# A dilated and sliding attention with a squared-ReLU FFN on one core: another order of the first loads, of the first batch's preparation and of the second layer's first groups

## Chip, core and metric

The kernel runs on 1 core of a Trainium2 chip. The metric is the device time of one execution in microseconds (us). Before the change the median of 5 runs is 316.51 us (316.03 to 317.87).

## What is computed

Two stages follow each other. First attention over 8 batches, 8 heads, 576 positions of 64 elements. Heads 0 to 3 see a plain causal window of 32 positions; heads 4 to 7 see 32 positions at a distance of 4 ("dilated"). Then the 4608 x 512 result goes through an FFN with 2048 hidden units.

```python
rel = pos[:, None] - pos[None, :]
mask_plain = (rel >= 0) & (rel < 32)
mask_dil = (rel >= 0) & (rel < 128) & (rel % 4 == 0)
attn = softmax(where(mask, q @ k.T / 8, -1e9))       # heads 0-3 plain, 4-7 dilated
x = (attn @ v) as 4608 tokens x 512
out = (relu(x @ w_in) ** 2) @ w_out                  # w_in 512 x 2048, w_out 2048 x 512
```

## The kernel before

**Units of work.** A head pair is called `e` (0 and 1 plain, 2 and 3 dilated). Batches 0 and 1 are cut in two parts (part 0: positions 0 to 255, part 1: the rest). Attention writes x transposed into the ring `xT`, where the FFN reads it. The FFN runs in tiles of 256 tokens (the first four) and then 512. `ffn_groups` (line 645) makes the groups of a tile: first-layer groups (`mm1`, line 656, matmuls on line 667, ReLU on ScalarE on line 678, square on VectorE on line 679), and second-layer groups (`g2`, line 691, matmuls on line 699). A second-layer group is named by an output row block `m` of 128 tokens and a `part` 0 to 3; part c multiplies four blocks of the hidden units by chunk c of `w_out_sb`, so the group waits for that chunk's load. When part 3 of an m is done, ScalarE copies the sum out of PSUM (line 705) and SyncE issues the store (line 641).

**Who sets the order.** Everything is ordered by hand, and each engine runs its instructions in that order. The text `PROGRAM` (line 21) is cut at each "|"; the piece before the first bar runs ahead of all groups, and each later piece runs behind one group of the list `groups` (line 802). The codes:

- `L0:q…`, `L0:v…`, `L0:i0` to `i3`, `L0:o0` to `o3`: loads, all issued by GpSimd (POOL) into one queue. `L0:q001` is q and k of batch 0, part 0, pairs 0 and 1; `i` is a quarter of w_in (line 753), `o` a chunk of w_out (line 758). `L0:v1d`, `L0:v1p`, `L0:v1r` are the values of part 1: `d` the dilated pairs (line 184), `p` the plain pairs (line 178), and `r` the last 64 positions of the dilated pairs, block 8 (two small loads on line 197).
- `w22`, `W14`: so many matmuls on a zeroed tile (`idle`, line 465) of 256 and 128 columns. Nothing reads their results.
- `T C B S E P D L X M` with e and part: batch 0's attention (`first_step`, line 469): transposes of q and k on TensorE (T, line 495), copies out of PSUM (C), masks added by a matmul (B, line 536), scores (S, line 555), exponential on ScalarE (E, line 560), product with the values (P, line 586), sums for the denominator (D, line 602), logarithm and its exponential on ScalarE (L and X, lines 609 and 612), the product into `xT` on VectorE (M, line 619).
- `1q2`, `2v2` and the like: a step of a later batch (`step`, line 434). q and k are transposes into the PSUM pool `ps_a` of two buffers (line 235) with copies into `qT` or `kbd` (lines 248 to 265; q of a plain pair is copied by ScalarE, the others by VectorE); v copies dilated values from the staging tile to `vbd` on VectorE (line 207); a and b are scores, o and p the product with the values, whose result VectorE scales into `xT` on line 428.

**Around the change.** In the first piece P of the dilated pairs (part 0) stands ahead of the transposes of their part 1. `groups` is reordered for the first two tiles: first-layer groups of both in turns, and from group 16 on the second layer of tile 0 (m 0 parts 0 to 3, then m 1 parts 0 to 3), then of tile 1. Behind group 1 stand `P21 P31`, which need the block-8 values.

Of the kernel before, what the change touches and what calls it, by code (L numbers as in the profile page):

```python
# [18 lines left out]


PROGRAM = (
    "L0:q001 L0:q023 L0:q101 L0:q123 L0:v0d L0:v0p L0:i0 L0:v1d L0:i1 L0:v1p L0:v1r L0:i2 L0:i3 L0:o0 "
    "L1:q00123 L0:o1 L0:o2 L0:o3 w22 T00 C00a T10 C10a B00 B10 W2 S00 E00 W3 S10 E10 W14 T20q W9 T20k C20v T30 "
    "C30v B20 B30 W3 S20 E20 W3 S30 E30 T01 C01v T11 C11v B01 B11 W2 S01 E01 P20 P30 D20 D30 T21 C21v S11 L20 "
    "X20 E11 T31 C31v M20 B21 B31 P00 P10 D00 D10 L00 X00 M00 S21 E21 S31 E31 W8 | | P21 P31 D21 D31 L21 X21 "
    "M21 L31 X31 M31 | | P01 P11 D01 D11 L01 X01 M01 L11 X11 M11 | | | | | | | | | | | | z | | y L1:v0dp "
    "L1:q10123 L1:v1dpr | | | | L2:q00123 L2:q10123 1q1 1q3 | 1q2 | 1k2 | 1k1 1v3 | 1a2 | 1v2 1k0 1q0 | 1o2 | "
    "1a0 1a1 | 1k3 1o0 1o1 | 1a3 1Q0 | 1K0 1o3 | 1Q1 1K1 | 1Q2 | 1b0 | | 1Q3 1K2 L2:vwpdr L3:q00123 L3:q10123 "
    "| L2:x | | 2q0 | | 2k0 1V2 | 1b2 1p0 | 1b1 1V3 1K3 | | 1p2 1p1 | 2a0 1b3 | 2k1 2o0 2b0 1p3 | 2q1 2k2 L3:x "
    "| | 2q2 2p0 L3:vwpdr 2a1 | | | 2b1 | 2v2 2o1 2q3 2a2 | | 2p1 | 2k3 | 2b2 2o2 | 2v3 | 2a3 2p2 L4:q10123 | "  # L30
    "2b3 | 3k1 2o3 3q1 | | 3a1 L4:q00123 2p3 | 3k0 3k2 | | 3o1 | | | 3q0 3v2 | | | | 3a0 | 3b1 3k3 | | | 3p1 "
    "L4:x 3q2 L4:vwpdr | | 3b0 | 3a2 3q3 3o0 4k0 | | | 3o2 3b2 | | 3p0 3v3 | 4q1 3a3 | 3p2 4q2 4q0 | L5:q10123 "
    "3b3 | 3o3 | 4k1 | | L5:q00123 3p3 4k2 4k3 4a0 L5:vwpdr | | | 4b0 | | 4q3 | | 4o0 | | | 4a2 4v2 | 4b2 | "
    "4a3 L5:x 4a1 | 4o2 | | | 4p2 L6:q00123 4v3 | | 4b1 | | 4p0 | | 4p1 | 5q0 5k0 | 4b3 | | | | 4o1 | | 5k2 "
    "L6:q10123 4o3 | 5q2 5k1 | | 4p3 | 5q1 |"
)


# [25 lines left out]
def kernel(  # L64
# [36 lines left out]
    NF = DFF // P  # L101
# [690 lines left out]
    G = 2 * NF  # L792
# [5 lines left out]
    groups, steps = [], []  # L798
# [2 lines left out]

    head = groups[:G]
    groups[:NF] = [head[y] for y in (0, 1, 2, 3, 16, 17, 18, 19, 4, 5, 20, 21, 6, 7, 22, 23)]
    groups[NF:G] = head[8:16] + head[24:32]
    for b in range(5, B):
        at = {"a": (-2, 8), "b": (0, 8), "o": (3, 8), "p": (6, 8), "v": (-4, 8)}
        at = {**({"k": (-9, 4), "q": (-9, 4)} if b > 5 else {}), **at}
# [50 lines left out]
```

## Time and profile before

| | |
|---|---|
| median of 5 runs | 316.51 us |
| the profiled execution's own time | 316.51 us |
| its span in the profile | 314.7 us |
| outside the span | 1.8 us |
| TensorE busy | 301.4 us, 96% of the span |
| VectorE, ScalarE, GpSimd busy | 201.1, 194.1, 87.3 us |
| granted TensorE clock | 1.00 in every slice |

Times in the profile count from the start of the span. PE is TensorE, DVE VectorE, ACT ScalarE, POOL GpSimd, SP SyncE. In the timeline a line gives the start, the duration, engine, source line and operation, and in brackets how long the engine had been idle and what ended that. In the chain of waits a line gives what the end was waiting on at that time.

When the loads of the queue were issued and when they landed, by the trace's answers for each issue (us):

| load | issued | landed |
|---|---|---|
| last of q and k of batch 0 | 5.68 | 12.4 |
| dilated values, part 0 | 6.31, 6.92 | 12.6, 13.5 |
| plain values, part 0 | 7.55 to 10.93 | 13.6 to 14.2 |
| w_in 1st quarter | 11.78 | 17.2 |
| dilated values, part 1 | 12.70, 13.3 | 17.5, 18.0 |
| w_in 2nd quarter | 13.88 | 21.3 |
| plain values, part 1 | 14.63 to 16.7 | 21.5 to 22.4 |
| block-8 values (`v1r`) | 17.46, 18.1 | 22.5, 22.6 |
| w_in 3rd quarter | 18.65 | 26.3 |
| w_in 4th quarter | 21.59 | 28.9 |
| w_out chunk 0 | 22.33 | 31.3 |
| q and k of batch 1, part 0 | 22.86, 23.56 | 33.3, 34.7 |
| w_out chunks 1, 2, 3 | 24.2, 24.8, 25.3 | 36.4, 38.9, 41.4 |

### The profile page before, as it was taken

To read this page: it belongs to the slowest core of one execution; us is meant where nothing else is said; L and a number is where in the kernel's file an instruction comes from. 1 tells how busy PE (TensorE), PEld (TensorE's weight loads), DVE (VectorE), ACT (ScalarE), POOL (GpSimd) and SP (SyncE) were. 2 spreads that over 40 slices of the span, in tenths; PEclk is the share of its full clock that TensorE was granted. 3 is DMA by queue.
4 is the path that set the end of the run, shared out by engine and by line. 5 is a ranking of instruction groups with operands and counts; after the bars stand their busy time and mean duration, and the time that the engine had idled before them with its cause. 6 is when DMAs were issued, how large, how long until landed. Compare 5 with 4: busy or idle time off the path is not lost.

```text
span 314.7 us, 6843 instructions
## 1 busy us (share of the span) xinstructions
PE 301.4 (96%) x2582; PEld 190.2 (60%) x2614; DVE 201.1 (64%) x641; ACT 194.1 (62%) x416; POOL 87.3 (28%) x136
## 2 busy tenths in 40 slices
PE   8969989999999999999999999999999999999995
PEld 5769835867855555555589655555555555445443
DVE  6335588898987987994799469956895334104400
ACT  6348526877968965686468646864686456217511
POOL 8774378455183036501361041000000000000000
PEclk9999999999999999999999999999999999999999
DMA  8999999999989999994599985602200210121022
GB/s 106 149 184 200 213 166 144 212 147 202 165 107 206 147 133 149 146 209 44 88 146 126 129 145 109 117 3 67 69 0 2 68 68 2 32 68 35 0 67 67
DMA packets 79808, 34.91 MB, mean 111 GB/s; under 512 B 49824, under 2 KB 74784, under 8 KB 79776
## 3 DMA queue, kind: packets, MB, share of 16 engines
q0 software_dynamic: 47680, 18.36, 52.8%
q1 hardware_dynamic: 31952, 15.93, 25.0%
q8 instruction: 20, 0.33, 0.5%
q10 hardware_dynamic: 144, 0.20, 0.2%
q14 instruction: 12, 0.10, 0.1%
HBM read 36.90 MB, written 9.44 MB: 147 GB/s over the span
## 4 chain that ended last, share of the span: by engine, by line
PE 78%; DMA 9%; ACT 4%; POOL 3%; issue 2%; DVE 1%; ACTq 0%; POOLq 0%
PE pf L699 36%; PE pf L667 32%; DMA w_out_sb<-in_moe_w_out_dram 5%; PE po L413 3%; DMA w_in<-in_moe_w_in_dram 2%; PE pd L415 2%; DMA qb<-in_q_dram 2%; PE pa L304 2%; PE pa L310 1%; ACT h2T L678 1%; ACT qT L248 1%; PE pa L235 1%; POOL qb L161 1%; POOL kb L161 1%; ACT rec L417 1%
## 5 line engine op out<-in xcount | busy, mean ns | idle before, releaser
L667 PE MATMUL pf<-xT,w_in 128*128 128x256 bf16 (+1 forms) x758 | 132.7, 325 | 2.0 <-DVE xT L619 0.9
L699 PE MATMUL pf<-w_out_sb,h2T 128*128 128x512 bf16 (+1 forms) x570 | 131.2, 373 | 3.0 <-DMA w_out_sb<-in_moe_w_out_dram 1.4
L667 PEld LDWEIGHTS <-w_in 128*128 128x128 bf16 x768 | 82.3, 113 | 37.0 <-issue 2.4
L678 ACT ACTIVATE h2T<-pf 128x512 bf16<-128x512 f32 x144 | 83.8, 598 | 24.6 <-PE pf L667 23.8
L699 PEld LDWEIGHTS <-h2T 128*128 128x128 bf16 x592 | 54.2, 98 | 55.2 <-issue 2.3
L679 DVE TENSOR_TENSOR h2T<-h2T 128x512 bf16<-128x512 bf16 x144 | 58.0, 423 | 40.3 <-ACT h2T L678 38.7
L705 ACT COPY osb<-pf 128x512 f32<-128x512 f32 (+1 forms) x37 | 21.2, 573 | 46.0 <-PE pf L699 45.9
L178 POOL DMA_DIRECT2D vbd<-in_v_dram x40 | 28.2, 721 | 58.5 <-PE pd L415 49.4
L428 DVE TENSOR_TENSOR xT<-po,rec 128x288 bf16<-128x288 f32 (+2 forms) x52 | 23.7, 457 | 31.3 <-ACT rec L418 30.8
L417 ACT ACTIVATE rec<-pd 128x288 f32<-128x288 f32 (+2 forms) x52 | 21.5, 414 | 23.9 <-PE pd L415 23.1
L314 ACT ACTIVATE pt<-pa 128x352 bf16<-128x352 f32 (+6 forms) x56 | 27.6, 499 | 7.9 <-PE pa L310 4.1
L418 ACT ACTIVATE rec<-rec 128x288 f32<-128x288 f32 (+2 forms) x56 | 24.9, 445 | 1.8
L413 PEld LDWEIGHTS <-vbd 128*128 128x128 bf16 x286 | 17.0, 97 | 9.9 <-issue 0.9
L248 DVE COPY qT<-xx 64x288 bf16<-64x288 bf16 x80 | 19.8, 247 | 1.1
L252 DVE COPY kbd<-xx 64x288 bf16<-64x288 bf16 x40 | 18.8, 470 | 0.6
L161 POOL DMA_DIRECT2D qb<-in_q_dram x18 | 13.0, 723 | 20.2 <-DMA xx<-qb 17.2
L413 PE MATMUL po<-pt,vbd 128*128 128x96 bf16 (+3 forms) x263 | 18.0, 198 | 0.4 <-DVE xT L428 0.3
L191 POOL DMA_DIRECT2D vd<-in_v_dram x24 | 14.6, 629 | 8.1 <-DMA kb<-in_k_dram 4.8
L415 PE MATMUL pd<-pt,mk 128*128 128x96 bf16 (+5 forms) x158 | 16.3, 203 | 0.0
L161 POOL DMA_DIRECT2D kb<-in_k_dram x18 | 12.8, 711 | 2.7 <-DMA w_out_sb<-in_moe_w_out_dram 1.8
L304 PE MATMUL pa<-qT,kbd 128*128 128x96 bf16 (+2 forms) x146 | 12.2, 201 | 0.5 <-ACT qT L248 0.5
L197 POOL DMA_DIRECT2D vbd<-in_v_dram x16 | 9.7, 609 | 10.3 <-PE pd L415 7.4
(81 smaller groups left out, 232.2 us busy)
## 6 DMA issues: line engine op xcount, KB each, us to landing
out_dram<-osb SPq DMA_DIRECT2D x18, 128.0 KB, 3.4
qb<-in_q_dram POOLq DMA_DIRECT2D x7, 320.0 KB, 8.1
kb<-in_k_dram POOLq DMA_DIRECT2D x7, 320.0 KB, 9.2
vd<-in_v_dram POOLq DMA_DIRECT2D x32, 64.0 KB, 4.8
w_in<-in_moe_w_in_dram POOLq DMA_DIRECT2D x4, 512.0 KB, 7.3
w_out_sb<-in_moe_w_out_dram POOLq DMA_DIRECT2D x4, 512.0 KB, 13.2
qb<-in_q_dram POOLq DMA_DIRECT2D x7, 256.0 KB, 7.1
kb<-in_k_dram POOLq DMA_DIRECT2D x7, 256.0 KB, 8.8
```

The costliest lines, as they stand in the source:

```text
L161: nc.gpsimd.dma_start(t[0:n, part, hs, :], src[b, hs, t0 : t0 + RES * n, :].rearrange("h (p r) d -> p h (r d)", r=RES))
L178: nc.gpsimd.dma_start(dst[rows, e, i0:i1, rows], v[b, 2 * e + hl, 64 * i0 : 64 * i1, :].rearrange("(i p) d -> p i d", p=64),)
L248: copy(qT[rows, e, :, m0 : m0 + n].rearrange("p (c j) m -> p j c m", j=2)[:, jj, :, :], src)
L314: nc.scalar.activation(pt[:, off : off + n], ps[:, 0:n], ACT.Exp, scale=SCALE)
L413: nc.tensor.matmul(oo, vb[:, e, i, :], rh, start=(x == 0), stop=(x == len(mms) - 1), skip_group_check=True)
L417: nc.scalar.activation(rec[:, 0:n], d[:, 0:n], ACT.Ln)
L418: nc.scalar.activation(rec[:, 0:n], rec[:, 0:n], ACT.Exp, scale=-1.0)
L428: nc.vector.tensor_tensor(out=tok, in0=o if o is o3 else o[:, 0:n], in1=rec if o is o3 else rec[:, 0:n], op=ALU.mult)
L667: nc.tensor.matmul(acc[u][:, nt * x + y0 : nt * x + y1], w_in_sb[piece][:, kt, c0 : c0 + 509 : 4], xT[:, kt, t0 : t0 + y1 - y0], start=(kt ...
L678: nc.scalar.activation(hv, acc[u][:, :].rearrange("p (x n) -> p x n", x=per), ACT.Relu)
L679: nc.vector.tensor_tensor(out=hv, in0=hv, in1=hv, op=ALU.mult)
L699: nc.tensor.matmul(cur[m][:, c0:c1], h2[:, f, P * m : P * m + P], w_out_sb[:, f, c0:c1], start=(f == 0), stop=(f == NF - 1),)
```

## The change

Seven edits, all of order or of number:

1. `L0:v1r` is issued with `L0:v1d`, ahead of the second quarter of w_in, and no longer behind the plain values of part 1.
2. `L1:q00123` (q and k of batch 1, part 0) is issued behind w_out's chunks 1 and 2, ahead of chunk 3.
3. `w22` becomes `w21`, `W14` becomes `W5`, `W9` becomes `W10`.
4. `T21 C21v S11 E11 T31 C31v B21 B31` come ahead of `P20 P30 D20 D30 L20 X20 M20`.
5. The second layer of tile 0 runs m 0 parts 0 and 1, m 1 parts 0 and 1, m 0 parts 2 and 3, m 1 parts 2 and 3.
6. `2v2` moves from behind group 54 to behind group 56. On VectorE its two copies then stand behind the next product on line 428 instead of ahead of the one before it.
7. `3k1` moves from behind group 62 to behind group 61; no engine's order of instructions is altered by it.

```diff
-    "L0:q001 L0:q023 L0:q101 L0:q123 L0:v0d L0:v0p L0:i0 L0:v1d L0:i1 L0:v1p L0:v1r L0:i2 L0:i3 L0:o0 "
-    "L1:q00123 L0:o1 L0:o2 L0:o3 w22 T00 C00a T10 C10a B00 B10 W2 S00 E00 W3 S10 E10 W14 T20q W9 T20k C20v T30 "
-    "C30v B20 B30 W3 S20 E20 W3 S30 E30 T01 C01v T11 C11v B01 B11 W2 S01 E01 P20 P30 D20 D30 T21 C21v S11 L20 "
-    "X20 E11 T31 C31v M20 B21 B31 P00 P10 D00 D10 L00 X00 M00 S21 E21 S31 E31 W8 | | P21 P31 D21 D31 L21 X21 "
...
-    "| | 2q2 2p0 L3:vwpdr 2a1 | | | 2b1 | 2v2 2o1 2q3 2a2 | | 2p1 | 2k3 | 2b2 2o2 | 2v3 | 2a3 2p2 L4:q10123 | "
-    "2b3 | 3k1 2o3 3q1 | | 3a1 L4:q00123 2p3 | 3k0 3k2 | | 3o1 | | | 3q0 3v2 | | | | 3a0 | 3b1 3k3 | | | 3p1 "
...
+    "L0:q001 L0:q023 L0:q101 L0:q123 L0:v0d L0:v0p L0:i0 L0:v1dr L0:i1 L0:v1p L0:i2 L0:i3 L0:o0 L0:o1 L0:o2 "
+    "L1:q00123 L0:o3 w21 T00 C00a T10 C10a B00 B10 W2 S00 E00 W3 S10 E10 W5 T20q W10 T20k C20v T30 C30v B20 "
+    "B30 W3 S20 E20 W3 S30 E30 T01 C01v T11 C11v B01 B11 W2 S01 E01 T21 C21v S11 E11 T31 C31v B21 B31 P20 P30 "
+    "D20 D30 L20 X20 M20 P00 P10 D00 D10 L00 X00 M00 S21 E21 S31 E31 W8 | | P21 P31 D21 D31 L21 X21 M21 L31 "
...
+    "2p0 L3:vwpdr 2a1 | | | 2b1 | 2o1 2q3 2a2 | | 2p1 2v2 | 2k3 | 2b2 2o2 | 2v3 | 2a3 2p2 L4:q10123 | 2b3 3k1 "
+    "| 2o3 3q1 | | 3a1 L4:q00123 2p3 | 3k0 3k2 | | 3o1 | | | 3q0 3v2 | | | | 3a0 | 3b1 3k3 | | | 3p1 L4:x 3q2 "
...
-    groups[NF:G] = head[8:16] + head[24:32]
+    groups[NF:G] = [head[y] for y in (8, 9, 12, 13, 10, 11, 14, 15)] + head[24:32]
```

## Prediction

> **What bounds the kernel now.** I read the page's busy times first. TensorE does something in 96% of the span, so only its gaps and what it has to wait for can move the end:
>
> ```profile
> PE 301.4 (96%) x2582; PEld 190.2 (60%) x2614; DVE 201.1 (64%) x641; ACT 194.1 (62%) x416; POOL 87.3 (28%) x136
> ```
>
> Then the list of what TensorE waited for in the first 60 us, and the chain of waits there:
>
> ```profile
> PE po L586 <- DMA vbd<-in_v_dram: 1.8, 1, 1.8
> PE pf L699 <- DMA w_out_sb<-in_moe_w_out_dram: 1.4, 1, 1.4
> ```
>
> ```profile
> 25.32 16.09 DMA w_out_sb<-in_moe_w_out_dram
> 41.41 0.04 issue
> 41.45 2.75 PE pf L699 x12
> ```
>
> The two largest waits are P21 for the block-8 values (20.9 to 22.7 us) and m 0 part 3 of tile 0 for w_out's chunk 3 (to 41.45 us). The chain says that only the second one sets the end: it goes from 41.41 us back along the load queue and never through the first. What happened on TensorE before 41 us matters only by what was left to do at 41.4 us. Now the timeline behind that moment:
>
> ```profile
> 41.45 2.75 PE L699 MATMUL pf<-w_out_sb,h2T 128*128 128x512 bf16 x12 [1.37 <-DMA w_out_sb<-in_moe_w_out_dram]
> ...
> 42.51 0.59 ACT L705 COPY osb<-pf 128x512 f32<-128x512 f32 x1 [4.39 <-PE pf L699]
> ...
> 44.04 0.45 PE L235 MATMUL pa<-mk,qb 80*128 80x80 bf16 x8
> ...
> 44.32 1.03 PE L699 MATMUL pf<-w_out_sb,h2T 128*128 128x512 bf16 x4
> 44.38 1.08 ACT L248 COPY qT<-pa 64x128 bf16<-64x128 bf16 x4 [1.28 <-PE pa L235]
> ...
> 45.51 0.30 PE L235 MATMUL pa<-mk,qb 80*128 80x80 bf16 x4 [0.16 <-ACT qT L248]
> ```
>
> Twelve matmuls are three groups (m 0 part 3, m 1 parts 0 and 1; 0.86 us each in the chain). Then come 1q1 and 1q3, one more group, and 1q2, which needs a `ps_a` buffer back and so waits for ScalarE's four copies of 1q1.
>
> **Part by part.**
>
> *Loads (edits 1 and 2).* The landings in the table come one behind the other from 17 us to 41 us, and the GB/s of the slices stay between 150 and 240 there: the queue is limited by what it moves. The bytes ahead of chunk 3 are the same after the change, so I take its landing at 41.4 us again. From 8.68 us on each POOL issue follows the landing of the load eight places before it (w_in's fourth quarter 21.59 after the second's 21.3; the first values of batch 1 26.56 after 26.3). With the new order the second quarter is issued at about 15.1 instead of 13.88 us, still 3 us before the loads ahead of it have landed (18.0), so no hole opens; POOL's later issues stay as far ahead of the queue as now. The block-8 values land at some 18.0 + 0.25 us (their two landings, 22.35 to 22.6) = 18.3 instead of 22.6 us, the second quarter at 21.6 instead of 21.3. Chunks 1 and 2 come 2.0 + 1.4 us earlier, near 33 and 35.5 us; q and k of batch 1 land near 38 and 39.4 us, before 1q1 wants them (42.3, below).
>
> *Fewer idle matmuls and the order of batch 0 (edits 3 and 4).* 14 idle matmuls took 0.78 us, 0.056 each. One less at the start gains nothing: the first transposes began at 5.32, and their k landed at 5.2. 9 less and 1 more are 8 x 0.056 = 0.45 us for all that follows (their q landed at 7.3, their k at 8.4 us, in time). T21, S11, T31 and B21 then run where TensorE waited 0.5 us for the values of part 0 (landed 13.5). ScalarE and VectorE set the rest, L20 to M00: D30 ends at about 14.55, then L20, X20, L00, X00 at some 0.62 us each and M00 0.69, so M00 ends near 17.85 instead of 18.79. First-layer work starts 0.9 us earlier. P21 starts at 19.5 and finds its values (18.3): the 1.8 us wait goes. Late next is w_in's second quarter: D31 ends at 20.9, u2 starts at 21.6 instead of 23.7. All that follows moves up by 2.1 us, and group 16 starts at 35.2 instead of 37.3 us.
>
> *Second layer (edit 5).* Before chunk 3 lands TensorE can now do five groups instead of three: 35.2 + 5 x 0.86 = 39.5 us. Then it waits 1.9 us for 41.4, longer than now. So all that edits 1, 3 and 4 gain is given back here; they serve only so that group 16 starts before 41.4 - 4.3 = 37.1 us, which today's 37.3 nearly does. After chunk 3 there are 2 groups fewer: 2 x 0.86 = 1.73 us by TensorE alone. But 1q1 now comes straight behind m 0 part 3, and its copies queue on ScalarE behind that block's copy-out. The copy-out starts at 42.51 as now; ScalarE's next start is 0.48 later (another copy-out at 51.11, its successor at 51.59); from there to 1q2 it is 45.51 - 44.38 = 1.13 us. So 1q2 starts at 42.51 + 0.48 + 1.13 = 44.12 instead of 45.51: **1.39 us** gained, and TensorE waits some 0.5 us in front of 1q2. Below VectorE runs almost without a pause from 1q2's copies on (45.85 to 51.8), so the shift is handed on as it is. Bounds: 1.73 if ScalarE does not hold it, 1.1 if the copy-out ends fully before the next starts (0.59) and chunk 3 comes 0.2 later.
>
> *2v2 and 3k1 (edits 6 and 7).* 3k1 alters no engine's order: nothing. For 2v2 the rows are:
>
> ```profile
> 85.13 0.60 DVE L207 COPY vbd<-vd 64x512 bf16<-64x512 bf16 x2
> ...
> 85.76 0.42 DVE L428 TENSOR_TENSOR xT<-po,rec 128x256 bf16<-128x256 f32 x1
> ...
> 86.24 0.38 PE L413 MATMUL po<-pt,vbd 128*128 128x32 bf16 x6 [0.35 <-DVE xT L428]
> ...
> 87.86 0.49 DVE L428 TENSOR_TENSOR xT<-po,rec 128x320 bf16<-128x320 f32 x1
> ...
> 88.57 0.34 PE L413 MATMUL po<-pt,vbd 128*128 128x96 bf16 x5
> ...
> 90.51 0.45 DVE L428 TENSOR_TENSOR xT<-po,rec 128x288 bf16<-128x288 f32 x1
> ...
> 91.01 0.33 PE L413 MATMUL po<-pt,vbd 128*128 128x96 bf16 x5
> ```
>
> The copies (0.63 us with their gaps) hold up the product at 85.76, whose denominators were ready at 85.48; without them TensorE's wait at 86.24 shrinks by 0.26. But the copies then run behind the product of 87.86 (87.6 after the shift), to 88.6, and 2o2 at 88.57 reads what they write: it waits about 0.35. The eight copies of 2k3 and the product of 90.51 move back by 0.35, and the matmuls of 91.01 need that product's buffer. Net +0.3 us. Bounds: -0.26 (if nothing behind is late) and +0.63 (all of it on the path). I take **+0.3**, by the chain just followed.
>
> *Sum.* 316.51 (this execution's own time, equal to the median) - 1.39 + 0.3 = **315.4 us**, 0.35% less.
>
> *The clock.* The granted clock is 1.00 in all slices, across the present gaps of 1.8 and 1.4 us. I count no loss for a 1.9 us gap. The Trainium skill, "TensorE: Matmul & The Clock Gate", section "HAM oscillation — how this bites in real kernels", speaks against longer gaps: it lets TensorE fall to half its clock when it is idle for more than about 3.4 us. By that rule the estimated 1.9 us is safe; if the gap grew past it, the next window would run at half speed, and the estimate from that page is a loss of 1.7 us, for 317.1.
>
> **The rivals.**
>
> *More comes through (314.5).* ScalarE's copies don't hold 1q2, and 2v2 gains its 0.26: 316.51 - 1.73 - 0.26 = 314.5. For it: the wait for ScalarE is only 0.16 us now. Against: the copy-out stood 1.9 us ahead of those copies and is now right in front of them.
>
> *Swallowed later (316.3).* VectorE is busy 16.6 of 18.8 us from 56 to 75 us and 21.2 of 25 from 75 to 100. If the 2v2 move costs its full 0.63, and VectorE loses as much again before the long tiles start at 94 us, 1.39 - 1.26 leaves 0.2: 316.3. Against: the chain from 45 to 75 us is mostly TensorE's own matmuls, and the loads there have slack (q of batch 2 landed at 54.8 and 58.9, used at 64.7).
>
> *Slower: chunk 3 lands late (317.4).* Place: the load queue. w_in's second and third quarters took 3.3 and 3.65 us between landings, the fourth 2.65: a weight load next to small value blocks or to q and k can cost 0.65 to 1.0 us more. If the new neighbours make two such (block 8 ahead of the second quarter, q and k ahead of chunk 3), chunk 3 lands 2.0 us later, and each us of that is a us of the end: 316.51 - 1.1 + 2.0 = 317.4. From a delay of 1.1 us on the kernel is slower than before. Against: the same loads in another order have the same neighbours in sum.
>
> **How the numbers follow.** Forecast (314.9 to 315.9): 0.50. More: 0.20. Swallowed: 0.22. Slower: 0.08. About 0.3%, 0.95 us, can be told from no change: faster means below 315.56. Of the forecast's 0.50 some 0.35 lies below that; with 0.20 and a little of the third case this is 0.57. Same: 0.15 + 0.20 = 0.36. Slower over 0.3%: 0.07, nearly all from the last rival. The range goes from the second case to the third with a margin of 0.3 for chunk 3's landing: 314.3 to 316.5.
>
> **What would show it.** After: TensorE's largest wait is in front of m 0 part 3, about 1.9 us, ending at 41.4; none at P21, a short one for w_in's second quarter near 21; the copy-out at 42.5 again; 1q2 at 44.1 behind a wait for ScalarE of about 0.5; a wait for line 207 near 87 us. The prediction is wrong if chunk 3 lands more than 0.5 us away from 41.4, if the distance from 1q2 to the span's end changes by more than 0.6 us, or if the granted clock falls anywhere.

## The result and the profile after

The changed kernel has a median of 315.95 us (46 executions, 314.09 to 319.48), the kernel before, on the same chips, 317.15 us (88 executions, 314.92 to 319.71). The ratio is 0.9963, 95% interval [0.995, 0.9975]: 0.37% or 1.2 us faster. Predicted were 315.4 us, 1.1 us less than the 316.51 us that the prediction started from; over 88 executions the kernel before has 317.15 us, so the measured 315.95 us lies above the predicted time although the difference agrees. The profiled execution of the changed kernel took 315.1 us with a span of 313.3 us, 1.4 us below that of before, with a mean granted clock of 0.999 (before 1.000).

The busy times hardly differ, so the gain must lie in gaps:

```profile
PE 301.8 (96%) x2573; PEld 190.1 (61%) x2605; DVE 200.6 (64%) x641; ACT 194.3 (62%) x416; POOL 87.3 (28%) x136
```

What TensorE waited for in the first 60 us of the changed kernel (us in total, times, longest):

```profile
PE pf L667 <- DVE xT L619: 1.3, 3, 0.8
...
PE pf L699 <- DMA w_out_sb<-in_moe_w_out_dram: 0.7, 1, 0.7
PE pf L555 <- issue: 0.6, 1, 0.6
PE pa L235 <- ACT qT L248: 0.5, 1, 0.5
...
PE pf L667 <- DMA w_in<-in_moe_w_in_dram: 0.3, 1, 0.3
```

P21's wait of 1.8 us for the block-8 values is gone, and that for chunk 3 is 0.7 instead of 1.4 us, not 1.9 as predicted. The chain of waits of the changed kernel still comes from chunk 3, and behind it from ScalarE:

```profile
25.24 16.04 DMA w_out_sb<-in_moe_w_out_dram
41.32 1.04 PE pf L699 x4
42.38 0.59 ACT osb L705
...
43.99 0.30 PE pa L235 x4
```

The timeline of the changed kernel there (one group of the second layer is four matmuls; a few records are missing from the traces, so x19 stands for the 20 of five groups):

```profile
36.19 4.48 PE L699 MATMUL pf<-w_out_sb,h2T 128*128 128x512 bf16 x19
...
41.32 1.02 PE L699 MATMUL pf<-w_out_sb,h2T 128*128 128x512 bf16 x4 [0.65 <-DMA w_out_sb<-in_moe_w_out_dram]
...
42.18 0.45 PE L235 MATMUL pa<-mk,qb 80*128 80x80 bf16 x8
42.38 0.59 ACT L705 COPY osb<-pf 128x512 f32<-128x512 f32 x1 [5.39 <-PE pf L699]
...
42.86 1.08 ACT L248 COPY qT<-pa 64x128 bf16<-64x128 bf16 x4
...
43.99 0.30 PE L235 MATMUL pa<-mk,qb 80*128 80x80 bf16 x4 [0.49 <-ACT qT L248]
```

Chunk 3 landed at 41.28 us (before 41.41). Behind it come four matmuls instead of twelve, 1q1 and 1q3, the copy-out and ScalarE's four copies, and 1q2 starts at 43.99 instead of 45.51: 1.52 us earlier. That shift is handed on: 1.51 us at group 56, 1.57 us at 2p2 (91.01 before, 89.44 after), 1.4 us at the end. From 1q2 to the end of the span it is 269.2 us before and 269.3 after.

### The profile page after: what moved, and what is told of

Read it like the earlier page. It is cut to its first block, busy times and chain, and to the rows that moved or that the text cites. A ratio compares the mean times of both kernels' runs of the same rounds, so it can differ in the third digit from the quotient of the medians.

```text
span 313.3 us, 6824 instructions
## 1 busy us (share of the span) xinstructions
PE 301.8 (96%) x2573; PEld 190.1 (61%) x2605; DVE 200.6 (64%) x641; ACT 194.3 (62%) x416; POOL 87.3 (28%) x136
## 4 chain that ended last, share of the span: by engine, by line
PE 77%; DMA 10%; ACT 5%; POOL 3%; issue 2%; DVE 2%; ACTq 0%; POOLq 0%
PE pf L699 36%; PE pf L667 32%; DMA w_out_sb<-in_moe_w_out_dram 5%; PE po L413 3%; DMA w_in<-in_moe_w_in_dram 2%; PE pd L415 2%; DMA vd<-in_v_dram 2%; PE pa L304 2%; PE pa L310 1%; ACT h2T L678 1%; ACT qT L248 1%; POOL qb L161 1%; POOL kb L161 1%; PE pa L235 1%; ACT rec L417 1%
## 5 line engine op out<-in xcount | busy, mean ns | idle before, releaser
L705 ACT COPY osb<-pf 128x512 f32<-128x512 f32 (+1 forms) x37 | 21.2, 574 | 47.0 <-PE pf L699 46.9
L252 DVE COPY kbd<-xx 64x288 bf16<-64x288 bf16 x40 | 18.8, 471 | 0.6
```

## The experiments

The theory is the prediction's: chunk 3's landing is a fixed point, work ahead of it counts only if it keeps TensorE from arriving late, and edit 5 gains by leaving less behind it. Each expectation states its rivals. Ratios are to the kernel before, run on the same chip beside it, with 95% intervals. The diffs of `PROGRAM` show only the codes around a difference, without the line breaks of the text; "..." stands for codes that are the same. In the expectations e2 is the kernel of "all but edit 5".

**Edit 5 alone** (before with the new second-layer order):

```diff
-    groups[NF:G] = head[8:16] + head[24:32]
+    groups[NF:G] = [head[y] for y in (8, 9, 12, 13, 10, 11, 14, 15)] + head[24:32]
```

> The kernel before with edit 5 alone (second layer of tile 0 in the new order). Theory A (the landing of w_out's chunk 3 at 41.3 to 41.4 us is fixed, and only what is left to do behind it moves the end): group 16 starts at 37.3 us as before, five groups end at 41.6, chunk 3 is no longer waited for or by less than 0.2 us, 1q2 starts at 44.2 instead of 45.51, and the time is 1.0 to 1.4 us (0.3 to 0.45%) below the kernel before, nearly all of the change. Theory B (the earlier preparation of batch 0 and the earlier block-8 values carry the gain): less than 0.3 us below the kernel before.

Measured: 0.9972 [0.995, 0.9993], 316.39 us against 317.36. So edit 5 brings a gain by itself. But 5 of 12 executions had a mean granted clock below 0.9975, and these had a median of 317.35 us, the others 315.86. The profiled one is of the first kind. Its windows from P21's wait on (length, then busy time and count of PE, PEld, DVE, ACT and POOL, then the granted clock, DMA share and GB/s):

```profile
20.90:22.70 1.80, 0.04 (x3) 0.05 (x1) 0.42 (x1) 0.27 (x1) 1.16 (x2) 1.00 1.35 191
22.70:24.00 1.30, 1.30 (x23) 0.94 (x24) 0.00 (x0) 0.06 (x1) 1.30 (x3) 0.63 1.09 144
24.00:25.00 1.00, 1.00 (x8) 0.76 (x7) 0.08 (x1) 0.97 (x3) 1.00 (x3) 0.50 1.15 179
25.00:26.00 1.00, 1.00 (x6) 0.74 (x5) 0.66 (x2) 0.68 (x2) 1.00 (x3) 0.50 1.22 197
26.00:27.00 1.00, 1.00 (x9) 0.83 (x7) 0.53 (x2) 0.60 (x1) 0.45 (x1) 0.77 1.31 238
```

Behind a pause of 1.8 us TensorE ran at half clock for some 3.5 us (a "dip" below). The sum had no term for that. One such stretch takes about 0.0055 off the mean clock of a span of 316 us (half of 3.5 in 316), so by this estimate a mean of 0.995 is one dip and 0.989 two.

**All but edit 5** (the changed kernel with the old line):

```diff
-    groups[NF:G] = [head[y] for y in (8, 9, 12, 13, 10, 11, 14, 15)] + head[24:32]
+    groups[NF:G] = head[8:16] + head[24:32]
```

> The changed kernel with the second layer of tile 0 in the old order. Theory A: group 16 starts at 36.2 us as after the change, three groups can be done ahead of chunk 3, the wait for chunk 3 is 41.3 - 36.2 - 2.6 = 2.5 us, 1q2 is at 45.4, and the time equals the kernel before within 0.2 us. Theory B: 1.0 us or more below the kernel before.

Measured: 1.0062 [1.0037, 1.0087], 319.56 us: slower than before, which neither theory had foreseen. 11 of 12 executions had a mean clock below 0.9975, four of them 0.989 or less. TensorE arrives early, waits long for chunk 3, and the twelve matmuls behind it are slow. Timeline, then windows, of this kernel:

```profile
41.83 4.18 PE L699 MATMUL pf<-w_out_sb,h2T 128*128 128x512 bf16 x12 [3.50 <-DMA w_out_sb<-in_moe_w_out_dram]
```

```profile
38.30:41.80 3.50, 0.03 (x1) 0.00 (x0) 3.12 (x4) 0.00 (x0) 1.35 (x2) 1.00 1.40 186
41.80:43.00 1.20, 1.17 (x6) 0.57 (x6) 0.61 (x2) 0.11 (x1) 0.92 (x2) 0.99 1.08 108
43.00:44.00 1.00, 1.00 (x4) 0.30 (x3) 0.00 (x0) 0.48 (x1) 1.00 (x3) 0.50 1.46 193
44.00:45.00 1.00, 1.00 (x4) 0.33 (x3) 0.00 (x0) 0.00 (x0) 1.00 (x2) 0.50 0.90 89
45.00:46.00 1.00, 1.00 (x6) 0.44 (x5) 0.00 (x0) 0.00 (x0) 1.00 (x3) 0.50 1.12 130
46.00:47.00 1.00, 1.00 (x12) 0.67 (x10) 0.41 (x2) 0.66 (x3) 1.00 (x3) 0.80 1.15 132
```

The same twelve took 2.75 us in the profile of before and 4.18 here.

**The clock as the cause**: the same kernel with 50 idle matmuls in that wait, which keep TensorE from pausing.

```diff
-    L1:q10123 L1:v1dpr | | | | L2:q00123
+    L1:q10123 L1:v1dpr | W50 | | | L2:q00123
```

> e2 (all edits but the new second-layer order) with 50 idle matmuls of 128 columns ahead of the group that waits for chunk 3. They write a PSUM tile that nobody reads. Clock theory (the pause of 3.5 us in front of chunk 3 let the granted clock fall to 0.50 for 3.5 us behind it, and that is why e2 took longer than the kernel before): the pause shrinks to under 1 us, the twelve matmuls behind chunk 3 take 2.75 us and not 4.18, the clock stays at 1.00, and the time falls by 1.5 to 3 us to the kernel before, 316.5 to 317.4. Rival (e2 is slow for another reason, a later landing of chunk 3 through the changed loads): the time stays within 0.5 us of e2.

Measured: 1.0013 [0.9985, 1.004], 318.04 us, 1 of 12 executions at the lower clock. That is 1.5 us less than without the idle matmuls, but above the 316.5 to 317.4 us expected. Timeline of the stretch:

```profile
41.05 2.95 PE L465 MATMUL pf<-idle 128*128 128x128 bf16 x50
43.84 2.75 PE L699 MATMUL pf<-w_out_sb,h2T 128*128 128x512 bf16 x11
```

The matmuls behind the filler are back at 2.75 us, against 4.18 without it: 1.43 us, which is nearly all of the 1.5. The rival, a late chunk 3, is out: the time fell, although in the profiled execution chunk 3 landed at 42.2 us, later than the 41.8 without the filler. The 1.0013 does not say that the other edits come to nothing, for 11 of the 19 executions of the kernel before beside it had a dip themselves. The executions without one have medians of 317.99 us with the filler and 316.85 before. Why these 1.1 us remain is not shown; the filler can cost time itself, as in the profiled execution, where it ended 1.6 us after the landing. That execution is also the one with a dip, in another place:

```profile
23.30 3.48 PE L667 MATMUL pf<-xT,w_in 128*128 128x256 bf16 x16 [1.62 <-DMA w_in<-in_moe_w_in_dram]
```

With the block-8 values ahead of it w_in's second quarter landed at 23.25 us here (21.3 in before). TensorE waited for it instead of for the block-8 values, and from 24 to 26 us the clock was 0.50.

**Edit 1 alone** (before, `L0:v1dr` ahead of the second quarter):

```diff
-    L0:v1d L0:i1 L0:v1p L0:v1r
+    L0:v1dr L0:i1 L0:v1p
```

> The kernel before with edit 1 alone (block-8 values ahead of w_in's second quarter). The prediction's chain of waits: TensorE gains 1.8 us at P21 and gives it back in front of chunk 3, time equal to the kernel before within 0.2 us. Clock theory (a pause of 1.8 us or more lets the granted clock fall to 0.50 in part of the executions, and the longer the pause the more often): the pause at P21 goes, but the one in front of chunk 3 grows from 1.4 us to 2.5 to 3.5 us, as in e2; the clock falls behind chunk 3 in most executions, with nothing left to hide it, and the time is 1 to 2 us above the kernel before.

Measured: 1.0009 [0.998, 1.0038], 318.09 us as the median of all twelve executions, of which 8 had the lower clock. The ratio leaves out the two longest (320.17 and 319.82 us, mean clock 0.989). With them the median is 0.9 us above that of before (317.16), so the expected loss of 1 to 2 us is neither shown nor excluded. In the profiled execution the dip cost little, and its timeline shows why:

```profile
39.52 1.86 PE L699 MATMUL pf<-w_out_sb,h2T 128*128 128x512 bf16 x4 [1.83 <-DMA w_out_sb<-in_moe_w_out_dram]
41.57 3.39 PE L699 MATMUL pf<-w_out_sb,h2T 128*128 128x512 bf16 x12 [0.19 <-DMA w_out_sb<-in_moe_w_out_dram]
```

Here chunks 1 and 2 come behind q and k, as in before, and TensorE pauses 1.83 us for chunk 2. Half the slow stretch (1.86 us for four matmuls, 1.02 at full clock) lies in time that would have been spent waiting for chunk 3; only 0.64 us of it (3.39 instead of 2.75 us) stands behind the landing.

**Edits 1 and 5** (before with both diffs above):

> The kernel before with edits 1 and 5 alone. Both theories: these two are the change; the time equals the changed kernel within 0.3 us (ratio to the kernel before 0.995 to 0.998). Clock theory besides: the share of executions with a granted clock under 0.997 is no larger than in the changed kernel (11 of 46) and smaller than with edit 5 alone (5 of 12, by the pause at P21). If edits 2, 3, 4, 6 carry a part, it is 0.5 us or more above the changed kernel.

Measured: 0.9953 [0.9929, 0.9977], 315.58 us, 0 of 12 executions at the lower clock. These two edits give what the whole change gives, as far as the intervals tell. Edit 5 alone (0.9972) can't be told from them by its time either; what edit 1 adds shows in the dips, 0 of 12 executions against 5 of 12. Timeline:

```profile
41.39 1.02 PE L699 MATMUL pf<-w_out_sb,h2T 128*128 128x512 bf16 x4 [0.96 <-DMA w_out_sb<-in_moe_w_out_dram]
...
44.06 0.30 PE L235 MATMUL pa<-mk,qb 80*128 80x80 bf16 x4 [0.49 <-ACT qT L248]
```

**Without edit 2** (the changed kernel, q and k of batch 1 between `L0:o0` and `L0:o1` again):

```diff
-    L0:o0 L0:o1 L0:o2 L1:q00123 L0:o3
+    L0:o0 L1:q00123 L0:o1 L0:o2 L0:o3
```

> The changed kernel with edit 2 undone (q and k of batch 1 ahead of w_out's chunks 1 and 2). Prediction: nothing, equal to the changed kernel within 0.2 us: chunks 1 and 2 land near 36.4 and 38.9 us and are wanted near 37.1 and 39.6, chunk 3 lands when it did. If chunk 2 becomes the late load, TensorE waits once more, in front of m 0 part 2, and the time is 0.3 to 0.8 us above the changed kernel.

Measured: 0.9958 [0.9933, 0.9983], 316.01 us, 0 of 12 executions at the lower clock. The wait is only split: 1.39 us in front of the first group that needs chunk 1 and 1.25 us in front of chunk 3's. Edit 2 is worth nothing that can be measured.

**Without edits 3 and 4** (the changed kernel with the old first piece):

```diff
-    w21 ... W5 T20q W10 ... E01 T21 C21v S11 E11 T31 C31v B21 B31 P20 P30 D20 D30 L20 X20 M20 P00
+    w22 ... W14 T20q W9 ... E01 P20 P30 D20 D30 T21 C21v S11 L20 X20 E11 T31 C31v M20 B21 B31 P00
```

> The changed kernel with the idle matmuls and the order of batch 0 as before (edits 3 and 4 undone). Theory A: P21 still finds its values, so group 16 starts by 36.5 us, five groups end ahead of chunk 3, and the time equals the changed kernel within 0.2 us. Theory B: it gives back 0.5 us or more. What this tells besides: the prediction had M00 0.9 us earlier by edits 3 and 4, and the trace after the change has it 0.2 us later; if those edits are worth nothing on their own, group 16 starts here at 36.0 to 36.2, no later than with them.

Measured: 0.9956 [0.9933, 0.998], 315.88 us, 2 of 12 at the lower clock. As good as the change. Group 16 even starts earlier (35.39 us, 36.19 in the changed kernel), but that follows w_in's second quarter, which landed at 21.7 us here and at 22.5 there:

```profile
35.39 4.48 PE L699 MATMUL pf<-w_out_sb,h2T 128*128 128x512 bf16 x19
42.88 1.02 PE L699 MATMUL pf<-w_out_sb,h2T 128*128 128x512 bf16 x4 [3.00 <-DMA w_out_sb<-in_moe_w_out_dram]
```

Chunk 3 landed late in this execution (42.8 us), and the pause of 3.00 us had no slow clock behind it: four matmuls in 1.02 us. With 316.77 us this execution is 0.9 us above the kernel's median: a late chunk 3 costs time by itself.

**Without edit 6** (the changed kernel, `2v2` back behind group 54):

```diff
-    | 2o1 2q3 2a2 | | 2p1 2v2 |
+    | 2v2 2o1 2q3 2a2 | | 2p1 |
```

> The changed kernel with 2v2 behind group 54 again. By the prediction it gains 0.3 us on the changed kernel. By the trace after the change (shift of 1.51 us at group 56, 1.56 behind 2p2) it loses 0.05 us, which can't be told from nothing: the wait of 0.35 us for line 428 in front of 2p1 is back, and the one of 0.19 for line 207 in front of 2o2 is gone. Also to be read: the eight copies of 2k3 on VectorE took 1.95 us before the change and 1.4 after; if it is GpSimd's issuing of loads next to them that makes them slow (it lay beside all eight before, beside six after), they take more than 1.6 us where it lies beside all of them again.

Measured: 0.994 [0.9915, 0.9964], 315.81 us, 3 of 12 at the lower clock. The interval overlaps that of the change: the move of `2v2` can't be told from nothing. The eight copies of 2k3 lay beside GpSimd's issues throughout and took 1.50 us (89.56 to 91.06), not more than 1.6: that GpSimd's issuing alone makes them slow is not borne out. The profiled execution is one with a dip. Chunk 3 landed at 43.0 us, and four matmuls behind it took 1.62 instead of 1.02 us:

```profile
43.04 1.62 PE L699 MATMUL pf<-w_out_sb,h2T 128*128 128x512 bf16 x4 [2.31 <-DMA w_out_sb<-in_moe_w_out_dram]
```

**Beyond the change.** Three kernels try what the theory suggests: bring the fixed point forward, or put work into the wait. The first loads chunk 3 ahead of q and k:

```diff
-    L0:o2 L1:q00123 L0:o3
+    L0:o2 L0:o3 L1:q00123
```

> The changed kernel with w_out's chunk 3 loaded ahead of q and k of batch 1. Theory A (TensorE waits for chunk 3 and for nothing else there): chunk 3 lands by 38 to 39.5 us, the wait in front of m 0 part 3 (0.65 us in the profiled execution, 2 to 3 us where chunk 3 landed near 43) goes, 1q1 finds q and k (landed near 41) and 1q2 comes 0.6 to 0.8 us earlier than after the change, at 43.3; no pause of TensorE over 1 us is left there, so the granted clock stays at 1.00. Time 0.6 to 1.5 us below the changed kernel. Rival C (q and k become the late load in its place): 1q1 waits for them until 41.5 or later, and the time equals the changed kernel within 0.3 us.

Measured: 0.989 [0.9844, 0.9936], 313.75 us, 0 of 6 at the lower clock. Timeline:

```profile
35.43 5.34 PE L699 MATMUL pf<-w_out_sb,h2T 128*128 128x512 bf16 x23
40.61 0.45 PE L235 MATMUL pa<-mk,qb 80*128 80x80 bf16 x8
...
42.42 0.30 PE L235 MATMUL pa<-mk,qb 80*128 80x80 bf16 x4 [0.49 <-ACT qT L248]
```

Chunk 3 landed at 38.3 us and q and k by 40.8. Six groups run through with no wait at all, and 1q2 is 1.6 us earlier than in the changed kernel. This version beats both kernels.

The second leaves the loads and moves 1q1, 1q3 and 1q2 two groups forward, ahead of chunk 3's group. `y` and `z`, zeroing on VectorE (`y` that of rows which the transposes read), move forward too:

```diff
-    | | | | | | | | | | | | z | | y L1:v0dp L1:q10123 L1:v1dpr | | | | L2:q00123 L2:q10123 1q1 1q3 | 1q2 | 1k2
+    | | | | | | | y | | | | z | | | L1:v0dp L1:q10123 L1:v1dpr | | 1q1 1q3 | 1q2 | L2:q00123 L2:q10123 | | 1k2
```

> The changed kernel with the first transposes of batch 1 moved into the wait for chunk 3 (1q1 and 1q3 behind group 19, 1q2 behind group 20), and VectorE's zeroing for batch 1 moved ahead (y behind group 9, z behind 13). Theory A: behind chunk 3's landing (41.3) only three groups are left without any wait between them; ScalarE's copies of 1q1 run ahead of the first copy-out, the wait of 0.49 us in front of 1q2 goes, and what was at 44.12 comes at 43.1: 1.0 us below the changed kernel. Rival (ScalarE's and VectorE's copies are the longer chain): 1q2 still comes late and holds chunk 3's group back; nothing gained.

Measured: 0.9907 [0.9875, 0.994], 315.01 us, 0 of 9 at the lower clock. The profiled execution, with a span of 311.2 us, was the fastest of the nine, and chunk 3 landed early in it (40.4 us), so its timeline shows the best case:

```profile
38.85 0.45 PE L235 MATMUL pa<-mk,qb 80*128 80x80 bf16 x8
...
40.33 0.30 PE L235 MATMUL pa<-mk,qb 80*128 80x80 bf16 x4 [0.16 <-ACT qT L248]
40.49 2.75 PE L699 MATMUL pf<-w_out_sb,h2T 128*128 128x512 bf16 x12
```

ScalarE's copies now lie beside groups that don't need chunk 3. The third does both, with 1q1, 1q3 and 1q2 one group forward instead of two:

```diff
-    L0:o2 L1:q00123 L0:o3
+    L0:o2 L0:o3 L1:q00123
...
-    | | | | | | | | | | | | z | | y L1:v0dp L1:q10123 L1:v1dpr | | | | L2:q00123 L2:q10123 1q1 1q3 | 1q2 | 1k2
+    | | | | | | | y | | | | z | | | L1:v0dp L1:q10123 L1:v1dpr | | | 1q1 1q3 | L2:q00123 L2:q10123 1q2 | | 1k2
```

> The two before in one: chunk 3 ahead of q and k, 1q1 and 1q3 behind group 20, 1q2 behind group 21, the zeroing ahead. Theory A: no wait over 0.3 us on TensorE from 36.2 to 44 us, state of 44.12 reached at 42.9: 1.2 us below the changed kernel where chunk 3 lands at 41.3 there, more where it lands later. Rival C: q and k land late (41.5 to 43) and 1q1 waits for them; less than 0.5 us.

Measured: 0.9896 [0.9855, 0.9937], 314.26 us, 0 of 6 at the lower clock. No more than the first of the three: the transposes now wait for q.

```profile
41.51 0.45 PE L235 MATMUL pa<-mk,qb 80*128 80x80 bf16 x8 [1.35 <-DMA qb<-in_q_dram]
```

## Why the prediction was right, and where it was not

*Chunk 3 and edit 5: right, with the right mechanism.* Chunk 3 landed at 41.28 (predicted 41.4), the copy-out started at 42.38 (42.5), ScalarE held 1q2 for 0.49 us (0.5), and 1q2 started at 43.99 (44.12). The term of 1.39 us measured 1.52, of which 0.13 is chunk 3's earlier landing. Edit 5 alone and edits 1 and 5 together confirm it by their times, the second also by its timeline.

*Edits 3 and 4: wrong.* M00 was to end at 17.85; it ended at 19.00 (before 18.79). The step that failed is "T21, S11, T31 and B21 then run where TensorE waited 0.5 us": they take more than that gap, and S11 stopped in its middle. Changed kernel:

```profile
12.99 0.30 PE L555 MATMUL pf<-xx 64*64 64x32 bf16 x6
13.87 0.30 PE L555 MATMUL pf<-xx 64*64 64x96 bf16 x6 [0.58 <-issue]
...
15.06 0.44 PE L586 MATMUL po<-pt,vd 64*64 64x64 bf16 x16
...
18.31 0.69 DVE L619 TENSOR_TENSOR xT<-pa,rec 128x512 bf16<-128x512 f32 x1 [0.46 <-ACT rec L612]
```

In before, all of P20 but its first matmul, and M00:

```profile
13.54 0.53 PE L586 MATMUL po<-pt,vd 64*64 64x64 bf16 x15 [0.46 <-DMA vd<-in_v_dram]
...
18.10 0.69 DVE L619 TENSOR_TENSOR xT<-pa,rec 128x512 bf16<-128x512 f32 x1 [1.28 <-ACT rec L612]
```

P20 starts at 15.06 instead of 13.54, and the chain from L20 to M00 hangs on it. What held S11 for 0.58 us the profile does not show ("issue"). It is not the whole delay: in the kernel without edit 2 S11 ran through, and P20 still began at 14.5. The late M00 did not delay group 16, though, because TensorE then waited for a load:

```profile
22.57 1.94 PE L667 MATMUL pf<-xT,w_in 128*128 128x256 bf16 x16 [0.34 <-DMA w_in<-in_moe_w_in_dram]
```

*Loads: near, with one term too small.* The block-8 values landed at 18.8 and 19.0 (predicted 18.3), w_in's second quarter at 22.5 (21.6), chunks 1 and 2 at 33.6 and 36.7 (33, 35.5), q and k at 38.1 and 39.4 (38, 39.4). The prediction gave the block-8 values 0.25 us of the queue; here they landed 1.7 us behind the dilated values (17.3). So the second quarter came 0.9 us late, and with it the first-layer group that waits for it (u2, 22.57 instead of 21.6). That put group 16 at 36.19 instead of 35.2 and made the wait for chunk 3 0.65 instead of 1.9 us. In the other kernels with edit 1 where the second quarter landed between 21.2 and 21.8 us, group 16 starts between 35.2 and 35.7, with the old order of batch 0 (edit 1 alone, without edits 3 and 4) as with the new. It cost nothing, since chunk 3 covers it, as the prediction had said of all gains ahead of it.

*2v2: the term of +0.3 was mis-sized; it measured about 0.* The chain is there, but 2o2's wait for line 207 was 0.19 instead of 0.35 us, and what should have handed it on did not: the eight copies of 2k3 (lines 259 and 265) took 1.4 us (87.14 to 88.56), in before 1.95 (88.27 to 90.22). Before, the first and the last of them:

```profile
88.27 0.21 DVE L259 COPY kbd<-xx 64x256 bf16<-64x256 bf16 x1
...
89.78 0.44 DVE L265 COPY kbd<-xx 64x32 bf16<-64x32 bf16 x1
```

Changed kernel:

```profile
86.51 0.60 DVE L207 COPY vbd<-vd 64x512 bf16<-64x512 bf16 x2
...
87.16 0.35 PE L413 MATMUL po<-pt,vbd 128*128 128x96 bf16 x5 [0.19 <-DVE vbd L207]
...
88.38 0.18 DVE L265 COPY kbd<-xx 64x32 bf16<-64x32 bf16 x1
...
88.85 0.45 DVE L428 TENSOR_TENSOR xT<-po,rec 128x288 bf16<-128x288 f32 x1
...
89.44 0.34 PE L413 MATMUL po<-pt,vbd 128*128 128x96 bf16 x5
```

The matmuls of 91.01 moved to 89.44, 1.57 us, where 1.52 had come in at 1q2. Why the copies were shorter stays open: slow ones stand only beside DMA issues of POOL, but not beside all of them.

*The clock and edit 1: wrong in the step "I count no loss for a 1.9 us gap", and in holding that edit 1 only readies group 16.* Of 83 executions of the kernel before that ran beside the experiments 48 had a mean clock below 0.9975 (median 317.70 us, the others 316.67); the profiled one was of the others. In before a dip thus costs 1.0 us, with edit 5 alone 1.5 (317.35 against 315.86). The likely reason is that the wait for chunk 3 hides part of a dip behind P21's pause, and edit 5 uses that cover up; no execution of before with a dip was profiled, so this is argued and not shown. Edit 1 takes P21's pause away: with edits 1 and 5 no execution of 12 had a dip. The change keeps some, 12 of 46 executions (317.39 us against 315.65). In its own profile there is none, but two related kernels show where they can come from: behind a wait of 2.31 us for chunk 3 (without edit 6) and behind one of 1.62 us for w_in's second quarter (with the filler). At full clock the two kernels differ by 316.67 - 315.65 = 1.0 us; the rest of the 1.2 us goes with the rarer dips.

*So the agreement of the sum is in part luck.* The sum of -1.1 us came out (-1.2), but with a term of +0.3 that wasn't there (2v2) and without one for the clock. At full clock the executions differ by 1.0 us, less than the 1.52 us that the profiled pair shows at 1q2; that pair is one draw of each kernel, and chunk 3's landing differs from execution to execution. Of the prediction's own signs, the wait of 1.9 us for chunk 3 (0.65) and the unchanged clock were not met, and chunk 3 landed more than 0.5 us from 41.4 in other executions (42.8, 43.0). The slower rival named something real: chunk 3 did land late in single executions, at 0.9 us of cost in one. But it didn't decide the result, and it lacked the danger that all but edit 5 showed, TensorE's own wait with half the clock behind it. In the rival "swallowed later", 1.39 - 1.26 leaves 0.13, hence 316.4 and not 316.3.

The Trainium skill, "TensorE: Matmul & The Clock Gate", section "HAM oscillation — how this bites in real kernels", has TensorE at half its clock after an idle gap of more than about 3.4 us; the table of the same page under "What's actually happening" has it need about 3.4 us of sustained work to come back. The depth and the length agree with the windows above (0.50, some 3.5 us); the threshold does not: here pauses of 1.62, 1.76, 1.83, 2.31 and 3.50 us had a dip behind them, and one of 3.00 us had none.

## What to carry over

When a load's landing ends a wait, count what is queued behind it on every engine, and take from there; what is gained ahead of it is given back, unless the load itself moves forward. A pause of TensorE costs more than its own length when the clock falls behind it, and a later wait may be hiding that: whoever removes the later wait must look at the earlier pause too. One profiled execution shows one draw; look at the granted clock of all executions before costing a gap at nothing.

## What was not expected of the hardware

- Pauses of 1.6 to 3.5 us let the granted clock fall to 0.50 for some 3.5 us in part of the executions: 11 of 12 with a 3.5 us wait in front of chunk 3, 48 of 83 in before with its 1.8 and 1.4 us, but only 2 of 12 where the profile shows 3.0 us (without edits 3 and 4). Where the longest wait in the profile is 1.4 us or less there were none in 45 executions of five kernels, but 12 in 46 of the changed kernel. With edit 5 alone a dip cost 1.5 us, and in all but edit 5 idle matmuls in the wait took as much back.
- The landing of chunk 3 differed between profiled executions with the same bytes ahead of it: 40.4 to 43.0 us, twice the whole effect of this change.
